# Linear attention and MLP, two layers of each: the denominators' reciprocals of later token chunks spread over the heads by 32-row products

## The chip, the core and the metric

The kernel runs on one core of a Trainium2 chip. The core has five engines with instruction queues of their own: TensorE (PE in the profile; its weight loads are PEld), VectorE (DVE), ScalarE (ACT), GpSimd (POOL) and SyncE (SP, which here issues the transfers). TensorE writes its products into PSUM, in banks of 512 fp32 columns; ScalarE and VectorE take them out to SBUF. The metric is the device time of one execution, in microseconds.

## What is computed

Four layers over x (2048 tokens, 576 features): A, B, A, B, each with a layer norm ahead of it and a residual sum behind it. A is linear attention with 32 heads of 18 features, B is an MLP of width 4608 with a GELU (it normalizes a second time). Cut from the reference:

```python
phi = lambda t: jnp.where(t > 0, t + 1, jnp.exp(t)) + 1e-6
pq, pk = phi(q), phi(k)
kv = jnp.einsum("bhsd,bhse->bhde", pk, v)
z = jnp.einsum("bhsd->bhd", pk)
num = jnp.einsum("bhqd,bhde->bhqe", pq, kv)
den = jnp.einsum("bhqd,bhd->bhq", pq, z)[..., None] + 1e-6
o = num / den                       # then heads side by side, times wo
...
x = x + _A_ref(_layernorm(x, axis=-1), A_wqkv, A_wo)
x = x + _B_ref(_layernorm(x, axis=-1), B_w1, B_b1, B_w2, B_b2)
```

The inputs are bfloat16, and the kernel's products take bfloat16 operands.

## The kernel before, in words

Tokens lie in 16 row tiles of 128, which make four chunks of 512. The 32 heads lie in five groups (`G`): four of 7 heads (126 features) and one of 4 heads (72). The change lies in the last part of layer A (`layer_A`, li = 0 and 2), the output loop at L827 to L846, and in the statistics of the rows that this loop hands to layer B.

*What stands ready ahead of the loop.* `kvwo[g]` holds kv times wo of a group, so that one product per group turns queries into output. The queries are made by `q_proj(g, c)` (L582): five products of 512 columns into one bank, an Exp and an Identity pass of ScalarE, then two VectorE instructions write phi(q) transposed, features by tokens, into `pq[(g, c)]`.

*Denominators.* `den_stage(c)` (L746) makes the denominators of a chunk with 20 products of 32 columns of weights: row tile j of the chunk goes to partitions 32j to 32j+31 (one row a head), 128 tokens along the columns. ScalarE takes Ln and then Exp with a scale of -1, which leaves the reciprocals in `rden` (128x128, one buffer).

*Spread over the heads' features.* `quad_stage(c)` (L765) copies `rden` four times beside each other through a mask, so that row tile j's heads are the only nonzero rows in the j-th 128 columns. `scale_stage(g, c)` (L775) multiplies by the 0/1 matrix `head_bc[:, g, :]`: one full product of 128 rows and 512 columns into a bank, a ScalarE copy to a tile `rden_bc`, and a VectorE multiply of `pq[(g, c)]` by it. This is done for five groups and four chunks.

*Output.* `wo_stage(t)` (L787) makes a row tile's output: ten products of 288 columns (five groups, two halves) into a pair of banks, `accA` and `accB` in turn. `residual` (L501) adds the old x on VectorE (L515) and issues the store of the row tile. SP issues the store, and the loads of old rows by `prefetch_xo`, in the order in which the planner placed them.

*Statistics for layer B.* The first four row tiles go on to layer B's first chunk by way of `LNPipe` (L301), a pipeline whose items move one stage with each `tick`; `hold` delays an item by so many ticks, and the loop ticks twice per row tile up to t = 9. With `stats="act"` ScalarE makes two passes over the row (L333, L340, the group `ln_dump` in the profile); with the default VectorE makes them (`bn_stats`, L349 and L350, and two small instructions). GpSimd makes the power of -1/2, the bias and the normalized row; TensorE then transposes it (L421), not before the output tile `tp_at`, and ScalarE copies it to `yT` (L428).

*What sets the order.* TensorE's instructions in this part are chained in the order of the program text (`pe`, L138). The other engines' orders come from a planner, bound by data and by the orderings without a wait (`add_manual_dep(..., NOSYNC, ...)`). Four PSUM banks, the ring `ps_h`, serve query groups, denominators, spreads and transposes in turn; a new user waits until the user of four places earlier has been read.

`turned` (L110) is an SBUF buffer of 2304 bfloat16 elements a partition, through which layer B's and the next layer's rows are transposed; it is not used during the output loop.

Of the kernel before, what the change touches and what calls it, by code (L numbers as in the profile page):

```python
# [7 lines left out]
ACT = mybir.ActivationFunctionType  # L8
ALU = mybir.AluOpType
BF16 = mybir.dt.bfloat16  # L10
F32 = mybir.dt.float32
# [3 lines left out]
S, D, F, H, DH = 2048, 576, 4608, 32, 18  # L15
P = 128
# [12 lines left out]
CA = 512  # L29
NCA = S // CA  # L30
# [4 lines left out]
def build(tc, A_x, A_wqkv, A_wo, B_w1, B_b1, B_w2, B_b2, out, dbg=None, n_layers=4):  # L35
    nc = tc.nc
    dbg = dbg or {}
    with ExitStack() as ctx:
        const = ctx.enter_context(tc.tile_pool(name="const", bufs=1))
        ps_h = ctx.enter_context(tc.tile_pool(name="ps_h", bufs=4, space=PSUM))  # L40
# [18 lines left out]
        head_bc = const.tile([P, G, P], BF16, name="head_bc")  # L59
# [50 lines left out]
        turned = const.tile([P, D // 32, TPC, 32], BF16, name="turned")  # L110
# [6 lines left out]
        rows = ctx.enter_context(tc.tile_pool(name="rows", bufs=9))  # L117

        def row_tile(name):
            return rows.tile([P, D], F32, name=name, tag="row")  # L120
# [3 lines left out]
        NOSYNC = mybir.DependencyInfo(mybir.DependencyClass.NoSync, mybir.DependencyReason.SCHED_ONLY)  # L124
# [13 lines left out]
        def pe(inst):  # L138
            if pe_chain["on"]:
                if pe_chain["last"] is not None:  # L140
                    tc.add_manual_dep(inst.ins, pe_chain["last"], NOSYNC, reason="TensorE order in the MLP")
                pe_chain["last"] = inst.ins.name
            return inst
# [76 lines left out]
        dve_last = dict(norm=None, sum=None, phi=None)  # L220
# [80 lines left out]
        class LNPipe:  # L301
# [11 lines left out]
            def tick(self, transposes=1):  # L313
                land()
                for it in list(self.items):
# [8 lines left out]
                    if st == -1:  # L324
                        xn = row_tile("xl")
# [4 lines left out]
                    elif st == 0 and it["stats"] == "act":  # L330
                        mv = it["mv"] = work.tile([P, 2], F32, name="ln_mv", bufs=6)
                        it["dump"] = blk.tile([P, D], BF16, name="ln_dump", tag="blk")
                        nc.scalar.activation(out=it["dump"][:], in_=it["xt"][:, 0:D], func=ACT.Identity,  # L333
                                             scale=-1.0 / D, accum_out=mv[:, 0:1])
                        it["stage"] = 0.5
                        continue
                    elif st == 0.5:
                        u = it["u"] = work.tile([P, 1], F32, name="ln_u", bufs=4)
                        mv = it["mv"]
# [6 lines left out]
                    elif st == 0:  # L346
                        xt = it["xt"]
                        stt = work.tile([P, 2, 6], F32, name="ln_st", bufs=4)
                        first = nc.vector.bn_stats(out=stt[:, 0, :], in_=xt[:, 0:HALF])  # L349
                        second = nc.vector.bn_stats(out=stt[:, 1, :], in_=xt[:, HALF:D])  # L350
                        after = dve_last["sum"] if it["after"] == "sum" else it["after"]
# [3 lines left out]
                        mv = work.tile([P, 2], F32, name="ln_mv", bufs=6)  # L355
# [23 lines left out]
                    elif st in (2, 3):  # L379
# [4 lines left out]
                        xt = it["xt"]  # L384
                        if it["norm"] == "act":
                            nc.scalar.activation(out=y[:, 0:D], in_=xt[:, 0:D], func=ACT.Identity,
                                                 scale=it["rstd"][:, 0:1], bias=it["nmr"][:, 0:1])
# [12 lines left out]
                        if it["kind"] == "A" and it["evac"] == "dma":  # L400
                            c, j = divmod(it["t"], TPC)
# [4 lines left out]
                    elif st == 4:  # L406
                        y = it["y"]
                        t = it["t"]
# [6 lines left out]
                        first = it["kind"] == "A" and t < 2  # L415
# [7 lines left out]
                        if first:  # L423
                            act_last["turned"] = nc.scalar.copy(out=yT[:, 0:3, t * P:(t + 1) * P], in_=tp[:, 0:3, :]).ins.name
                            copy = nc.vector.tensor_copy(out=yT[:, 3:KD, t * P:(t + 1) * P], in_=tp2[:, 3:KD, :])
# [16 lines left out]
        lnp = LNPipe()  # L442
        act_last = dict(exp=None, gelu=None)
# [81 lines left out]
        def layer_A(li, next_kind, pre_a1=None):  # L525
# [3 lines left out]
            pq = {}  # L529
# [67 lines left out]
            q_left = [(g, c) for c in range(NCA) for g in range(G)]  # L597
            pe_chain["on"] = True
            kvwo = {}
            if li > 0:  # L600
# [87 lines left out]
                for g in range(G):  # L688
                    pe(nc.tensor.matmul(zp[0:GR[g], g:g + 1], lhsT=k2[4][:, GO[g]:GO[g] + GR[g]], rhs=ident[:, 64:65],
                                        start=True, stop=True))  # L690
# [30 lines left out]
            if li == 0:  # L721
# [5 lines left out]
                                    in1=zp[0:126, 0:4].unsqueeze(2).to_broadcast([126, 4, H]), op=ALU.mult)  # L727
            nc.vector.tensor_tensor(out=zsel[0:72, 4, :], in0=head_sel[0:72, 4, :],
                                    in1=zp[0:72, 4:5].to_broadcast([72, H]), op=ALU.mult)
# [12 lines left out]

            quad_rden = {}
            rden_of = {}

            def den_stage(c, after=None, pair=None):  # L746
                if pair:
                    dp = ps_acc.tile([P, 2, 512], F32, name="den_pair", tag=pair)[:, 0, :]
                else:
                    dp = ps_h.tile([P, 512], F32, name="den_ps", tag="h")  # L750
                for g in range(G):
                    rows = 127 if g == 0 else GR[g]
                    for j in range(TPC):
                        pe(nc.tensor.matmul(dp[32 * j:32 * (j + 1), 0:P], lhsT=zsel[0:rows, g, :],
                                         rhs=pq[(g, c)][0:rows, j * P:(j + 1) * P],
                                         start=(g == 0), stop=(g == G - 1)))
                rden = work.tile([P, P], BF16, name="rden", bufs=1)
                log = nc.scalar.activation(out=dp[:, P:2 * P], in_=dp[:, 0:P], func=ACT.Ln)
                if after is not None:
                    tc.add_manual_dep(log.ins, after, NOSYNC, reason="copies first")  # L760
                act_last["rden"] = nc.scalar.activation(out=rden[:], in_=dp[:, P:2 * P], func=ACT.Exp,
                                                        scale=-1.0).ins.name
                rden_of[c] = rden

            def quad_stage(c, after=None):  # L765
                quad = blk.tile([P, D], BF16, name="quad_rden", tag="blk")
                spread_out = nc.vector.tensor_tensor(
                    out=quad[:, 0:CA].rearrange("p (j n) -> p j n", j=4), in0=quad_mask[:],
                    in1=rden_of.pop(c)[:].unsqueeze(1).to_broadcast([P, 4, P]), op=ALU.mult)
                if after is not None:  # L770
                    tc.add_manual_dep(spread_out.ins, after, NOSYNC, reason="sums first")
                quad_rden[c] = quad
                dve_last["quad"] = spread_out.ins.name

            def scale_stage(g, c, pair=None):  # L775
                if pair:
                    bp = ps_acc.tile([P, 2, 512], F32, name="rden_pair", tag=pair)[:, 0, :]
                else:
                    bp = ps_h.tile([P, 512], F32, name="rden_ps", tag="h")
                pe(nc.tensor.matmul(bp[:, 0:CA], lhsT=head_bc[:, g, :], rhs=quad_rden[c][:, 0:CA], start=True, stop=True))  # L780
                rb = blk.tile([P, D], BF16, name="rden_bc", tag="blk")
                act_last["copy"] = nc.scalar.copy(out=rb[0:GR[g], 0:CA], in_=bp[0:GR[g], :]).ins.name  # L782
                mult = nc.vector.tensor_tensor(out=pq[(g, c)][0:GR[g], 0:CA], in0=pq[(g, c)][0:GR[g], 0:CA],  # L783
                                               in1=rb[0:GR[g], 0:CA], op=ALU.mult)
                dve_last["mult"] = mult.ins.name

            def wo_stage(t):  # L787
                c, j = divmod(t, TPC)
                wp = ps_acc.tile([P, 2, 512], F32, name="wo_ps", tag=("accA", "accB")[t % 2])
                for half in range(2):  # L790
                    for g in range(G):
                        pe(nc.tensor.matmul(wp[:, half, 0:HALF], lhsT=pq[(g, c)][0:GR[g], j * P:(j + 1) * P],  # L792
                                              rhs=kvwo[g][0:GR[g], half * HALF:(half + 1) * HALF],
                                              start=(g == 0), stop=(g == G - 1)))
                xn = residual(li, t, wp[:, :, 0:HALF])
                if xn is not None and next_kind == "B" and t < TPC:
                    lnp.feed(xn, t, "B", "pool", "act", hold=1, stats="act", tp_at=6 + 2 * t)

            for t in range(AHEAD):
                prefetch_xo(li, t, add_b2=False)  # L800
# [9 lines left out]
            if li > 0:  # L810
                kv_groups((2, 3, 4))
                late = [q_proj(*q_left.pop(0), defer=True)]
            kv_wo(2)
            kv_wo(3)
            if li == 0:
                late = [q_proj(*q_left.pop(0), defer=True)]
# [10 lines left out]
            for t in range(NT):  # L827
                c, j = divmod(t, TPC)
                if t + AHEAD < NT:
                    prefetch_xo(li, t + AHEAD, add_b2=False)  # L830
                wo_stage(t)
                for late in list(rden_of):
                    quad_stage(late, after=dve_last["sum"])
                if q_left:
                    q_proj(*q_left.pop(0))
                if c + 1 < NCA:
                    for g in ((0, 1, 2), (3, 4), (), ())[j]:
                        scale_stage(g, c + 1)
                if j == 1 and c + 2 < NCA:
                    den_stage(c + 2)  # L840
                if t == NT - 3:
                    warm_table(ACT.Gelu_apprx_tanh, act_last["copy"])
                state["wo"] = t
                lnp.tick()
                if t < 10:
                    lnp.tick(transposes=0)  # L846
# [237 lines left out]
```

## Time and profile before

| | us |
|---|---|
| median of 3 runs (lowest to highest) | 768.49 (768.37 to 768.53) |
| the profiled execution | 768.48 |
| its span, first to last instruction | 766.7 |
| output loop of li = 0, from its first output product to the MLP's first | 77.68 to 107.32 |
| output loop of li = 2, likewise | 454.07 to 481.70 |
| in these two stretches together (57.26): TensorE busy | 55.80 |
| ScalarE busy | 45.22 |
| VectorE busy | 43.13 |
| GpSimd busy | 18.46 |

The granted TensorE clock is 1.00 in both stretches. A TensorE product's duration in the profile reaches into the time of the next one (a product of 288 columns lasts 286 ns, while products of this kind start 120 to 125 ns apart), so a stretch is read by the starts of its instructions. A line of a timeline has the start in us, the length of the group, engine, line of the kernel, operation, what it writes and reads, shapes, and how many instructions it groups; in brackets the idle time ahead of it and what ended it.

### The profile page before, as it was taken

To read this page: it belongs to the slowest core of one execution; us is meant where nothing else is said; L and a number is where in the kernel's file an instruction comes from. 1 tells how busy PE (TensorE), PEld (TensorE's weight loads), DVE (VectorE), ACT (ScalarE), POOL (GpSimd) and SP (SyncE) were. 2 spreads that over 40 slices of the span, in tenths; PEclk is the share of its full clock that TensorE was granted. 3 is DMA by queue.
4 is the path that set the end of the run, shared out by engine and by line. 5 is a ranking of instruction groups with operands and counts; after the bars stand their busy time and mean duration, and the time that the engine had idled before them with its cause. 6 is when DMAs were issued, how large, how long until landed. Compare 5 with 4: busy or idle time off the path is not lost.

```text
span 766.7 us, 15671 instructions
## 1 busy us (share of the span) xinstructions
PE 760.5 (99%) x6522; PEld 492.6 (64%) x6522; DVE 269.5 (35%) x669; ACT 341.5 (45%) x768; POOL 123.9 (16%) x202
## 2 busy tenths in 40 slices
PE   9999999999999999999999999999999999999998
PEld 6776664675477457646777767447745764674476
DVE  7786764035113603400455677600140032000000
ACT  5888956304710660164056578560065027205600
POOL 4681412012100301200110004300020011001000
PEclk9999999999999999999999999999999999999999
DMA  9992483016402721330246007530131033011000
GB/s 262 264 302 48 140 276 79 28 57 164 123 24 62 194 70 40 96 87 1 73 122 214 1 16 247 203 81 15 51 107 50 17 124 81 9 32 55 2 9 24
DMA packets 80289, 73.82 MB, mean 96 GB/s; under 512 B 36698, under 2 KB 64858, under 8 KB 80218
## 3 DMA queue, kind: packets, MB, share of 16 engines
q1 hardware_dynamic: 80218, 72.82, 32.3%
q8 instruction: 51, 0.84, 0.5%
q14 instruction: 20, 0.16, 0.1%
HBM read 48.03 MB, written 24.77 MB: 95 GB/s over the span
## 4 chain that ended last, share of the span: by engine, by line
PE 96%; ACT 3%; DVE 1%; issue 0%; DMA 0%; ACTq 0%
PE m_ps L965 36%; PE h_ps L907 20%; PE hp_ps L907 16%; PE q_ps L585 5%; PE wo_ps L792 3%; PE k_ps L537 3%; PE k_ps L608 3%; PE k_ps L625 2%; PE v_ps L558 1%; PE m_half L965 1%; PE v_ps L555 1%; ACT rden_bc L782 1%; PE tp L421 1%; ACT ln_dump L333 1%; PE kvacc L579 1%; PE k_tail L625 1%
## 5 line engine op out<-in xcount | busy, mean ns | idle before, releaser
L965 PE MATMUL m_ps<-w_sb,hT 128*128 128x288 bf16 x2232 | 274.8, 286 | 0.0
L965 PEld LDWEIGHTS <-hT 128*128 128x128 bf16 x2304 | 224.8, 98 | 59.8 <-issue 3.4
L907 PEld LDWEIGHTS <-w_sb 64*128 64x128 bf16 x2304 | 124.5, 94 | 136.4 <-issue 1.9
L907 PE MATMUL hp_ps<-yT,w_sb 64*128 64x512 bf16 x1152 | 178.0, 376 | 0.0
L907 PE MATMUL h_ps<-yT,w_sb 64*128 64x512 bf16 x1152 | 147.9, 376 | 0.0
L912 ACT COPY relay_sb<-relay_sb 128x1 f32<-128x1 f32 x144 | 28.6, 198 | 262.9 <-PE h_ps L907 220.0
L903 ACT ACTIVATE hT<-h_ps,b1T 128x512 bf16<-128x512 f32 x144 | 91.2, 684 | 43.8 <-PE h_ps L907 43.8
L372 POOL TENSOR_TENSOR ln_rstd<-ln_u,neg_half 128x1 f32<-128x1 f32 x64 | 36.2, 567 | 376.8 <-DVE ln_u L363 225.6
L903 ACT ACTIVATE hT<-hp_ps,b1T 128x512 bf16<-128x512 f32 x144 | 91.2, 693 | 0.0
L515 DVE TENSOR_TENSOR xbf<-m_ps,xo 128x576 bf16<-128x576 f32 x15 | 11.4, 758 | 214.5 <-PE m_ps L965 214.5
L515 DVE TENSOR_TENSOR xo<-m_ps,xo 128x576 f32<-128x576 f32 x16 | 12.1, 758 | 174.6 <-PE m_ps L965 174.6
L498 POOL TENSOR_TENSOR xo<-xo,b_bc 128x576 f32<-128x576 f32 x32 | 41.0, 1286 | 100.5 <-DMA xo<-x_d 63.6
L907 PE MATMUL h_ps<-yT,w_tail 64*128 64x512 bf16 x144 | 54.1, 376 | 0.0
L907 PE MATMUL hp_ps<-yT,w_tail 64*128 64x512 bf16 x144 | 54.1, 376 | 0.0
L585 PE MATMUL q_ps<-yT,wqkv_sb 128*126 128x512 bf16 (+1 forms) x200 | 49.8, 380 | 0.0
L792 PE MATMUL wo_ps<-kvwo,pq 126*128 126x288 bf16 (+1 forms) x320 | 43.4, 286 | 0.4
L907 PEld LDWEIGHTS <-w_tail 64*128 64x128 bf16 x288 | 27.1, 94 | 17.1
L792 PEld LDWEIGHTS <-pq 126*128 126x128 bf16 (+1 forms) x320 | 30.1, 97 | 10.7 <-DVE pq L783 0.9
L464 ACT ACTIVATE phi_e<-k_ps 128x288 bf16<-128x288 f32 x46 | 19.3, 419 | 38.7 <-PE k_ps L608 35.8
L585 PEld LDWEIGHTS <-wqkv_sb 128*126 128x126 bf16 (+1 forms) x200 | 24.9, 131 | 11.7 <-issue 0.4
L472 DVE TENSOR_SCALAR phi_e<-phi_e 128x288 bf16<-128x288 bf16 (+2 forms) x86 | 24.8, 288 | 19.9 <-ACT phi_e L464 19.2
L464 ACT ACTIVATE phi_e<-q_ps 126x512 bf16<-126x512 f32 (+1 forms) x40 | 23.9, 598 | 17.1 <-PE q_ps L585 16.8
(133 smaller groups left out, 665.4 us busy)
## 6 DMA issues: line engine op xcount, KB each, us to landing
xo<-x_d SPq DMA_DIRECT2D x48, 288.0 KB
x_d<-xo SPq DMA_DIRECT2D x32, 288.0 KB
xl<-x_d SPq DMA_DIRECT2D x24, 288.0 KB
y_d<-turned SPq DMA_DIRECT2D x40, 144.0 KB
w_sb<-in_B_w_dram SPq DMA_DIRECT2D x6, 864.0 KB
yT<-y_d SPq DMA_DIRECT2D x10, 512.0 KB
w_sb<-in_B_w_dram SPq DMA_DIRECT2D x9, 512.0 KB
x_d<-xn SPq DMA_DIRECT2D x16, 288.0 KB
```

The source lines that it names most:

```text
L372: nc.gpsimd.tensor_tensor(out=rstd[:], in0=it["u"][:], in1=neg_half[:], op=ALU.pow)
L464: exp = nc.scalar.activation(out=e_out, in_=ps_ap, func=ACT.Exp)
L472: low = nc.vector.tensor_scalar(out=e[0:rows, 0:n], in0=e[0:rows, 0:n], scalar1=1.0, scalar2=1e-6, op0=ALU.min, op1=ALU.add)
L498: nc.gpsimd.tensor_tensor(out=xo[:], in0=xo[:], in1=b2_bc[:], op=ALU.add)
L515: total = nc.vector.tensor_tensor(out=xn[:, cols].rearrange("p (h n) -> p h n", h=2), in0=halves, in1=xo[:, cols].rearrange("p (h n) -> p ...
L537: pe(nc.tensor.matmul(kp[:, 0:HALF], lhsT=yT[:, k, tok], rhs=wqkv_sb[:, k, D + half * HALF: D + (half + 1) * HALF], start=(k == 0), stop=( ...
L585: pe(nc.tensor.matmul(qp[0:GR[g], :], lhsT=wqkv_sb[:, k, GO[g]:GO[g] + GR[g]], rhs=yT[:, k, c * CA:(c + 1) * CA], start=(k == 0), stop=(k ...
L792: pe(nc.tensor.matmul(wp[:, half, 0:HALF], lhsT=pq[(g, c)][0:GR[g], j * P:(j + 1) * P], rhs=kvwo[g][0:GR[g], half * HALF:(half + 1) * HALF ...
L903: act_last["gelu"] = nc.scalar.activation(out=to, in_=ps, func=ACT.Gelu_apprx_tanh, bias=b1T[:, f:f + 1], scale=1.0).ins.name
L907: mm = pe(nc.tensor.matmul(dst[n], lhsT=wt, rhs=mv, start=(seen[n] == 0), stop=(seen[n] == 8)))
L912: relay = nc.scalar.copy(out=relay_sb[:, 1:2], in_=relay_sb[:, 0:1])
L965: pe(nc.tensor.matmul(acc[half][:, 0:HALF], lhsT=hT[f][:, j * P:(j + 1) * P], rhs=w2_sb[:, f, half * HALF:(half + 1) * HALF], start=(f == ...
```

## The change

1. *Spread.* For chunks 1 to 3 groups 0 to 3 are no longer spread by `scale_stage`. A new `quarter_stage(c)` multiplies `rden` directly: for each group and each quarter i of the partitions, a product of 32 rows and 128 columns, quarter i into bank i, all four banks of the ring at once. ScalarE then copies each bank into a part of `turned`. `quarter_scale` multiplies `pq` of a group by four runs of 128 columns from the four parts. Group 4 and all of chunk 0 keep `scale_stage`, and so `quad_stage` stays.
2. *Order.* The spread of chunk 1 stands after output tile 1, those of chunks 2 and 3 after tiles 3 and 7; the denominators of chunk 2 move from tile 1 to tile 2, those of chunk 3 stay at tile 5. Multiplies of `pq` and masked spreads are placed behind a row tile's residual sum.
3. *Statistics.* The first four row tiles' statistics start later (`hold` 4, 4, 6, 8 in place of 1). Those of tiles 1 and 3 go to VectorE behind the latest sum, those of tiles 0 and 2 stay on ScalarE behind the latest Exp of the denominators.
4. *Queries.* Query groups left for the loop (three in li = 0, one in li = 2) are not issued at tiles 1 and 3, where spreads stand.

```diff
@@ LNPipe.tick, statistics on ScalarE
-                        nc.scalar.activation(out=it["dump"][:], in_=it["xt"][:, 0:D], func=ACT.Identity,
-                                             scale=-1.0 / D, accum_out=mv[:, 0:1])
+                        one = nc.scalar.activation(out=it["dump"][:], in_=it["xt"][:, 0:D], func=ACT.Identity,
+                                                   scale=-1.0 / D, accum_out=mv[:, 0:1])
+                        if it["after"] == "rden":
+                            tc.add_manual_dep(one.ins, act_last["rden"], NOSYNC, reason="denominators first")
@@ den_stage
                 rden_of[c] = rden
+                rden_now["tile"] = rden
@@ new
+            def quarter_stage(c):
+
+                rden = rden_now["tile"]
+                banks = [ps_h.tile([P, 512], F32, name="rden_ps", tag="h") for _ in range(4)]
+                for g in range(4):
+                    for i in range(4):
+                        rows = slice(32 * i, 32 * (i + 1))
+                        pe(nc.tensor.matmul(banks[i][0:126, g * P:(g + 1) * P], lhsT=head_bc[rows, g, 0:126],
+                                            rhs=rden[rows, :], start=True, stop=True))
+                spread_rows = turned[:].rearrange("p a t c -> p (a t c)").rearrange("p (i w) -> p i w", i=4)
+                for i in range(4):
+                    act_last["copy"] = nc.scalar.copy(out=spread_rows[0:126, i, 0:4 * P], in_=banks[i][0:126, :]).ins.name
+
+            def quarter_scale(c, groups, after):
+                spread_rows = turned[:].rearrange("p a t c -> p (a t c)").rearrange("p (i w) -> p i w", i=4)
+                for g in groups:
+                    scaled = pq[(g, c)][0:126, 0:CA].rearrange("p (i n) -> p i n", i=4)
+                    mult = nc.vector.tensor_tensor(out=scaled, in0=scaled,
+                                                   in1=spread_rows[0:126, :, g * P:(g + 1) * P], op=ALU.mult)
+                    tc.add_manual_dep(mult.ins, after, NOSYNC, reason="sums first")
+                    dve_last["mult"] = mult.ins.name
@@ wo_stage
-                    lnp.feed(xn, t, "B", "pool", "act", hold=1, stats="act", tp_at=6 + 2 * t)
+                    lnp.feed(xn, t, "B", "pool", "act", hold=(4, 4, 6, 8)[t], tp_at=6 + 2 * t,
+                             **(dict(after="sum") if t % 2 else dict(stats="act", after="rden")))
@@ the output loop, behind wo_stage(t)
-                for late in list(rden_of):
-                    quad_stage(late, after=dve_last["sum"])
-                if q_left:
+                total = dve_last["sum"]
+                if c + 1 < NCA:
+                    for g in ((), (), (0, 1, 2, 3), ())[j] if c == 0 else ((0, 1), (2, 3), (), ())[j]:
+                        quarter_scale(c + 1, (g,), after=total)
+                    if t == 1:
+                        quarter_stage(1)
+                    if j == 3 and c + 2 < NCA:
+                        quarter_stage(c + 2)
+                    if j == (2 if c == 0 else 0):
+                        scale_stage(4, c + 1)
+                if j == (2 if c == 0 else 1) and c + 2 < NCA:
+                    den_stage(c + 2)
+                    if c > 0:
+                        quad_stage(c + 2, after=total)
+                if t == 3:
+                    quad_stage(2, after=total)
+                if q_left and t not in (1, 3):
                     q_proj(*q_left.pop(0))
-                if c + 1 < NCA:
-                    for g in ((0, 1, 2), (3, 4), (), ())[j]:
-                        scale_stage(g, c + 1)
-                if j == 1 and c + 2 < NCA:
-                    den_stage(c + 2)
```

More of the change, by code (lines that the diff above doesn't have):

```diff
@@ L744, in layer_A @@
             rden_of = {}
+            rden_now = {}
             def den_stage(c, after=None, pair=None):
```

## The prediction, made before the changed kernel ran

> **What bounds the kernel.** I read the page first: which engine is full, and what its chain of waits holds.
>
> ```profile
> PE 760.5 (99%) x6522; PEld 492.6 (64%) x6522; DVE 269.5 (35%) x669; ACT 341.5 (45%) x768; POOL 123.9 (16%) x202
> ...
> PE 96%; ACT 3%; DVE 1%; issue 0%; DMA 0%; ACTq 0%
> ```
>
> TensorE is the bound, but 3% of the chain stands on ScalarE. Comparing the two programs' instruction orders shows that the change touches only the output loops of the two attention layers (li=0: 77.68 to 107.32; li=2: 454.07 to 481.70), so I read TensorE's timeline there, li=2 first:
>
> ```profile
> 454.07 1.71 PE L792 MATMUL wo_ps<-kvwo,pq 126*128 126x288 bf16 x10
> 455.62 1.24 PE L585 MATMUL q_ps<-yT,wqkv_sb 128*72 128x512 bf16 x5
> ...
> 458.58 0.60 PE L780 MATMUL rden_ps<-quad_rden,head_bc 128*128 128x512 bf16 x2
> 459.11 0.47 PE L754 MATMUL den_ps<-pq,zsel 127*32 127x128 bf16 x20
> 459.50 4.11 PE L792 MATMUL wo_ps<-kvwo,pq 126*128 126x288 bf16 x30
> 463.45 0.81 PE L780 MATMUL rden_ps<-quad_rden,head_bc 128*128 128x512 bf16 x3
> ...
> 465.34 0.38 PE L780 MATMUL rden_ps<-quad_rden,head_bc 128*128 128x512 bf16 x1
> 466.17 0.38 PE L780 MATMUL rden_ps<-quad_rden,head_bc 128*128 128x512 bf16 x1 [0.46 <-ACT rden_bc L782]
> 466.66 0.47 PE L754 MATMUL den_ps<-pq,zsel 127*32 127x128 bf16 x20
> ```
>
> The starts matter, since each duration holds a tail that overlaps the next product. The paces: a broadcast (0.81−0.38)/2 = 0.216 us; a query group of five 1.08; a row tile's ten output products 1.235 (ten rows start that far apart elsewhere in the loop); five transposes 0.28. Against them the starts lose 0.32 before the first query group, 0.10 at 459.11, 0.25 within the 30 products, 0.61 between 465.34 and 466.17, 0.27 before 466.66: 1.55. In li=0 the same sum gives 1.5, of which again 0.32 stands before the loop's first steps and is not touched. ScalarE's timeline tells why:
>
> ```profile
> 464.11 0.79 ACT L340 ACTIVATE ln_dump<-xo,ln_mv 128x576 bf16<-128x576 f32 x1
> ...
> 464.87 0.69 ACT L333 ACTIVATE ln_dump<-xo 128x576 bf16<-128x576 f32 x1
> ...
> 465.53 1.56 ACT L782 CAST rden_bc<-rden_ps 126x512 bf16<-126x512 f32 x3
> ```
>
> Broadcasts issued from 463.45 on are evicted only from 465.53, behind passes over statistics. So about 1.2 us a layer is ScalarE's, and the rest of the loop is TensorE's own work.
>
> **Part by part.** *The spread.* Per later chunk (three a layer) four full 128-row products of 512 columns go: 4×0.216 = 0.86 us. In come 16 products of 32 rows and 128 columns, four row quarters into four banks. No 32-row product is in this trace. The nearest row is the denominators' 20, four column quarters wide and also 128 columns long:
>
> ```profile
> 76.97 0.38 PE L780 MATMUL rden_ps<-quad_rden,head_bc 128*128 128x512 bf16 x1
> 77.28 0.47 PE L754 MATMUL den_pair<-pq,zsel 127*32 127x128 bf16 x20
> 77.68 1.71 PE L792 MATMUL wo_ps<-kvwo,pq 126*128 126x288 bf16 x10
> ```
>
> Their starts spread over 0.47−0.22 = 0.25 us: five waves of four, 0.06 apart, so four run at once. From 76.97+0.216 to 77.68 the whole step takes 0.49, so about 0.20 goes at entering and leaving the quarter shape. Four waves then cost 0.24+0.20 = 0.44. That row quarters run at once too is carried by the MLP's 64-row halves (L907 in the page: 2,592 products of 512 columns, 560 us in a row at 0.216; the chain of waits gives them 20% and 16%, 276 us). Lower end 0.37, were the change of shape a third cheaper; upper ends in the rivals. I take 0.44: a saving of 0.42 a chunk, 6×0.42 = 2.5 us, all on the path.
>
> The Trainium skill, TensorE: Matmul & The Clock Gate, section "Wait — 56ns, not 53.3ns?", says that starts never come closer than about 25 ns; 16 starts would then take 0.40 and the step 0.60. The 13 ns above disagrees, and the measurement decides.
>
> *Evictions and multiplies.* ScalarE still makes four 126x512 copies a chunk (0.48 apart: (1.56−0.60)/2), into `turned` in place of four tiles; VectorE still makes five multiplies and one masked spread. I cost the multiplies alike at 0.34 apart (83.12 0.75 x2). Their new operand comes in four runs of 128; the masked spread, whose operand is also read in four runs, takes 0.43 like them. Not one multiply can start before all four copies are done, a new wait: that is in the walk below. Reuse of `turned` makes a chunk's copies wait for the last chunk's multiplies.
>
> *Statistics.* Of eight ScalarE passes a layer four go: 2×(0.67+0.76) = 2.9 us of ScalarE. VectorE gets two rows' statistics of about 1.2 us (two halves of 0.44, 0.21, 0.14). The remaining passes are held behind a denominators' Exp. *Queries* are not issued beside a spread; the group of five is moved, not changed. *SP* issues the same 308 transfers; in li=2 stores and loads change places and the load of row 10 waits for row 1's normalization; I place that near 467 with row 10 added near 473, so it has 4 us where its issue takes 0.32. GpSimd has no new work.
>
> *The walk.* All four PSUM banks of one ring go to a spread, and the next broadcast, denominators or query group must take them back in order, one copy at a time. I laid the new order out with these paces.
>
> li=2: first spread 457.93 (after two output tiles), copies 458.45 to 460.48, multiplies of chunk 1 to 461.95. Denominators 459.82, their Exp done 461.43; second spread enters 461.55; output tile 4 at 461.99, its operands ready. ScalarE makes the two passes first, copies of chunk 2 from 462.77: the single broadcast waits for a bank and the masked spread, 463.22 to 463.45, 0.23 lost. Third spread 468.15 (about 0.1 more lost on a sum), its copies 468.67 to 470.7, well ahead of tile 12 at 474.3. MLP at 479.6 in place of 481.70: 2.1 us less.
>
> li=0 has two more query groups in the loop. First spread 81.54, no wait; second 86.23, 0.1 for the last query bank. Chunk 2's copies start at 87.59 behind two query passes and two statistics passes; the broadcast loses 0.34, the query group 0.26, and the third denominators 0.18 for that query. MLP at 105.9 in place of 107.32: 1.4 us less.
>
> So the saving of 2.5 is joined by 2.3 us of old waits that end and eaten by 1.3 us of new ones (0.9 in li=0, 0.4 in li=2, rounded up): 2.5+2.3−1.3 = 3.5. The profiled execution took 768.48 (span 766.7 and 1.8 around it; the median shown is 768.49), so **765.0**. What comes late next is the bank ring, by ScalarE's four copies in a row. The MLP's input cannot be late: its last transposes stand three output tiles (3.7 us) ahead of it, as before. Own range of this case: 763.8 to 766.6, for 0.3 us a layer either way in bank waits and a spread of 0.37 to 0.60.
>
> **Rivals.**
> *All new waits vanish*: the gain is 2.5+2.3, 763.7, and with a spread of 0.37 763.3. For it, chunks 1 and 3 find their banks free in the walk; against it, chunk 2's copies stand behind 1.4 us of statistics. 0.10.
>
> *Loads do not hide within a row quarter*: each wave pays a load and then a product. A load of 126 columns is bounded by z_ps (L689, five one-column products in 0.47−0.20, 0.07 each), so a wave is 0.13, the spread 4×0.13+0.20 = 0.72, 6×0.28 = 1.7 us less gain: 766.7. Against it, the denominators' second wave of loads starts while the first wave's products run (20 loads busy 0.29 us in all). The Trainium skill's same page, section "The mechanism", has this rule: a load overlaps products in flight only in another row group. The trace's denominators, which use all rows, disagree. 0.12.
>
> *VectorE becomes the bound*: at the sums' rate (0.76 for 576 fp32) a strided multiply takes 0.60 apart. Twelve of them a layer push everything behind them back. In li=2 chunk 1's are done at 462.9 in place of 461.95 (tile 4 waits 0.55, the masked spread brings that to 0.85), and then the sums of tiles 5 and 6 hold tiles 7 and 8 up to 2.1 in all; in li=0 the third denominators wait 1.3 for a query. Together 3.4: 768.4, no change. The masked spread's 0.43 speaks against it. 0.10.
>
> *Slower: products in series.* If the four quarters do not overlap, 16 products go singly. At the pace of kv_ps (L645, 126 by 126, 0.0575) a spread is 1.12; 6×(1.12−0.86)−1.0 = +0.6: 769.1, 0.05. If load and product also follow each other, 0.13 each, the spread is 16×0.13+0.20 = 2.28: 6×1.42−1.0 = +7.5: 776.0, 0.10. It decides from a spread of about 1.03 us on, where 6×0.17 eats the 1.0 net of waits. For it: no row shows four row quarters at once. Against: the halves do overlap.
>
> **How the numbers follow.** Forecast 0.53, the rivals 0.10, 0.12, 0.10, 0.05, 0.10. The range 763.2 to 768.4 takes in all but the series (0.05+0.10). A measurement of this kernel tells about 0.2%, 1.5 us, from no change. Faster (below 767.0): 0.53+0.10 and most of 0.12, 0.74; same 0.16; slower 0.10.
>
> **What would show it.** The spread's 16 products start over some 0.2 us, and the next output product starts 0.44 after the last one's end; over 0.9 there means series. The MLP starts near 105.9 and some 25.6 us after 454.07. No broadcast waits behind `ln_dump`; waits in front of single broadcasts are for `turned` copies, 0.2 to 0.4 each. VectorE's multiplies from `turned` last 0.43; at 0.6 or more VectorE is the bound. If the spread shows 0.44 and the loops end no earlier, the bank ring has taken the gain.

## The result, and the profile after

| | before | after |
|---|---|---|
| median (lowest to highest, 6 runs each), us | 768.51 (768.33 to 768.66) | 771.94 (769.55 to 772.55) |
| the profiled execution, its span, us | 768.48, 766.72 | 769.55, 767.84 |
| loop of li = 0, first output product to the MLP, us | 29.64 | 28.78 |
| loop of li = 2, likewise, us | 27.64 | 29.59 |

The ratio is 1.0042, 95% interval 1.0032 to 1.0052. The change makes the kernel **slower by 0.4%**; the prediction was 765.0, faster, with a range up to 768.4. The loops account for the profiled execution: −0.86 and +1.95 make +1.09, and the span grew by 1.12. The other five executions of the changed kernel took 2.2 to 3.0 us more than the profiled one. All five had a mean granted clock of 0.996 to 0.998, the profiled one 1.000; that part is taken up below.

In the changed kernel the line numbers are other ones: output products are L818, the spread by quarters L798, broadcasts L784, the row sums L517; of the transfers, L524 is the store of a row tile and L495 the load of an old one. The first two fences are the busy times and the chain of waits of the page after:

```profile
PE 758.3 (99%) x6594; PEld 491.6 (64%) x6594; DVE 270.0 (35%) x685; ACT 336.9 (44%) x752; POOL 124.0 (16%) x198
```

```profile
PE 95%; DMA 2%; DVE 2%; ACT 1%; issue 0%; SPq 0%; DVEq 0%
```

ScalarE's share of the chain fell from 3% to 1%, which is what the change was forecast to do. In its place stand transfers (2%), which were at 0%. TensorE's timeline of li = 2 after the change shows where:

```profile
453.24 1.71 PE L818 MATMUL wo_ps<-kvwo,pq 126*128 126x288 bf16 x10
...
455.87 1.40 PE L818 MATMUL wo_ps<-kvwo,pq 126*128 126x288 bf16 x10
457.19 0.45 PE L798 MATMUL rden_ps<-rden,head_bc 32*126 32x128 bf16 x16
457.57 1.41 PE L818 MATMUL wo_ps<-kvwo,pq 126*128 126x288 bf16 x10
...
461.24 1.41 PE L818 MATMUL wo_ps<-kvwo,pq 126*128 126x288 bf16 x10
462.74 0.38 PE L784 MATMUL rden_ps<-quad_rden,head_bc 128*128 128x512 bf16 x1
...
474.86 0.44 PE L423 MATMUL tp<-ident,y_ring 128*128 128x128 bf16 x5
476.51 1.39 PE L818 MATMUL wo_ps<-kvwo,pq 126*128 126x288 bf16 x10 [1.20 <-DVE xo L517]
480.21 2.68 PE L818 MATMUL wo_ps<-kvwo,pq 126*128 126x288 bf16 x20 [2.31 <-DVE xo L517]
482.82 1.04 PE L943 MATMUL h_ps<-yT,w_sb 64*128 64x512 bf16 x8
```

Up to 474.86 the stretch runs as the walk had it. The spread takes 0.38 from its first start to the next output product, and some 0.09 at entry (455.87 to 457.19 is 1.32, where ten output products pace 1.235). Then TensorE stands still twice ahead of the last three output tiles (13, and 14 with 15), behind row sums on VectorE. No such wait was in the profile before. Starts show what each stop costs: the ten products at 476.51 could have begun 0.28 after the transposes at 474.86, so 1.37 is lost; those at 480.21 could have begun 1.235 after 476.51, so 2.47 is lost. Without these 3.84 the MLP would have begun at 478.98, 25.74 us after the loop's first product; the prediction said 25.6.

Why were the sums late? They add the *old* row, which has to be loaded first. SP's timeline of the changed kernel (stores L524 and loads L495, in SP's order; a time here is how long SP was held at the instruction):

```profile
459.80 2.73 SPq L524 DMA_DIRECT2D x_d<-xo  x2
464.53 3.67 SPq L495 DMA_DIRECT2D xo<-x_d  x2
468.29 0.85 SPq L524 DMA_DIRECT2D x_d<-xo  x2
472.51 0.32 SPq L495 DMA_DIRECT2D xo<-x_d  x1
472.88 0.90 SPq L524 DMA_DIRECT2D x_d<-xo  x2
473.88 1.26 SPq L495 DMA_DIRECT2D xo<-x_d  x2
```

The second line holds the loads of rows 9 and 10. Row 10's takes the buffer of row 1, which is free only when GpSimd has normalized row 1, at 467.8. SP works in order, so the stores of row tiles 4 and 5, whose sums end at 464.4 and 466.1, go out only at 468.29. Store 4 lands at 472.49; the load of row 11 takes that store's buffer and cannot go earlier than 472.51. Row 12's load takes the buffer of store 5, and stores 6 and 7 and the load of row 13 stand in the queue behind row 11's. From there the loads come close behind each other, as the chain of waits in order of time shows (excerpt):

```profile
468.29 4.20 DMA x_d<-xo
...
473.88 5.40 DMA xo<-x_d
...
480.21 2.68 PE wo_ps L818 x20
```

The load at 473.88 is row 12's; it lands 5.40 us after its issue. VectorE's timeline has the sums of rows 10, 11 and 12:

```profile
472.62 0.74 DVE L517 TENSOR_TENSOR xo<-wo_ps,xo 128x576 f32<-128x576 f32 x1
475.70 0.76 DVE L517 TENSOR_TENSOR xo<-wo_ps,xo 128x576 f32<-128x576 f32 x1 [2.33 <-PE tp L423]
479.39 0.76 DVE L517 TENSOR_TENSOR xo<-wo_ps,xo 128x576 f32<-128x576 f32 x1 [2.94 <-DMA xo<-x_d]
```

Row 10 itself is not late: its load goes out at 467.87, lands at 471.77, and its sum starts at 472.62 without a wait. Row 11's sum waits for its load, which lands at 475.62 (the bracket names the transposes, which had ended by 475.3), and row 12's for the load of 473.88.

The same seen from the transfers, in two stretches of li = 2 (columns: stretch and length, busy time and instructions of PE, PEld, DVE, ACT and POOL, granted clock, DMA share, GB/s). Before the change:

```profile
464.00:472.00 8.00, 7.43 (x78) 5.17 (x76) 6.11 (x11) 6.37 (x18) 6.77 (x16) 1.00 0.63 178
472.00:480.00 8.00, 8.00 (x72) 6.27 (x70) 5.88 (x11) 5.45 (x10) 0.97 (x2) 1.00 1.04 382
```

and after it:

```profile
464.00:472.00 8.00, 8.00 (x100) 6.00 (x99) 7.93 (x20) 7.28 (x16) 7.02 (x14) 1.00 0.48 147
472.00:480.00 8.00, 4.70 (x43) 3.60 (x41) 2.73 (x6) 1.97 (x4) 1.63 (x2) 1.00 0.80 233
```

Before, the transfers ran at a full share (1.04) in the last 8 us of the loop. After, they moved less in both stretches, and not for want of room. In slices of 0.4 us from 464.00 to 480.00 their busy share is, in tenths:

```profile
DMA  0003794000009269999400049489999965898999
```

They stand idle from 466.8 to 468.8, when SP waits for row 1, and from 472.0 to 473.2, when it waits for store 4. What is then released comes close together, and each load lands later than the one ahead of it: 3.1 us after its issue for row 11, 5.4 for row 12, 6.2 for row 13.

### The profile page after: what moved, and what is told of

Read it like the earlier page. It is cut to its first block, busy times and chain, and to the rows that moved or that the text cites. A ratio compares the mean times of both kernels' runs of the same rounds, so it can differ in the third digit from the quotient of the medians.

```text
span 767.8 us, 15791 instructions
## 1 busy us (share of the span) xinstructions
PE 758.3 (99%) x6594; PEld 491.6 (64%) x6594; DVE 270.0 (35%) x685; ACT 336.9 (44%) x752; POOL 124.0 (16%) x198
## 4 chain that ended last, share of the span: by engine, by line
PE 95%; DMA 2%; DVE 2%; ACT 1%; issue 0%; SPq 0%; DVEq 0%
PE m_ps L1001 36%; PE h_ps L943 20%; PE hp_ps L943 16%; PE q_ps L587 5%; PE wo_ps L818 3%; PE k_ps L539 3%; PE k_ps L610 3%; PE k_ps L627 2%; PE v_ps L560 1%; PE m_half L1001 1%; PE v_ps L557 1%; DMA xo<-x_d 1%; DMA wqkv_sb<-in_A_wqkv_dram 1%; PE tp L423 1%; DMA x_d<-xo 1%; PE kvacc L581 1%
## 5 line engine op out<-in xcount | busy, mean ns | idle before, releaser
L517 DVE TENSOR_TENSOR xbf<-m_ps,xo 128x576 bf16<-128x576 f32 x15 | 11.4, 758 | 212.7 <-PE m_ps L1001 212.7
L517 DVE TENSOR_TENSOR xo<-m_ps,xo 128x576 f32<-128x576 f32 x16 | 12.1, 758 | 173.7 <-PE m_ps L1001 173.7
L818 PE MATMUL wo_ps<-kvwo,pq 126*128 126x288 bf16 (+1 forms) x320 | 44.0, 286 | 3.8 <-DVE xo L517 3.5
L818 PEld LDWEIGHTS <-pq 126*128 126x128 bf16 (+1 forms) x320 | 29.8, 97 | 13.6 <-issue 3.8
```

Source lines behind the costliest of these rows:

```text
L517: total = nc.vector.tensor_tensor(out=xn[:, cols].rearrange("p (h n) -> p h n", h=2), in0=halves, in1=xo[:, cols].rearrange("p (h n) -> p ...
```

## Experiments

Two theories stood against each other. **A**: the loss is the place of stores 4 and 5 in SP's queue, behind the load that waits for row 1; the spread and the statistics do what the walk said. **B**: the spread, the multiplies or the statistics cost more than priced, and the row waits are only where it shows. A second question was why most executions lose another 2.2 to 3.0 us.

**The changed kernel once more, one execution.**

> The changed kernel as it is, for a trace of an execution whose granted clock falls. Theory A: the clock falls to a lower value within a few us of the row waits near 480, and the products after it run slower for some us; 771.5 to 772.5. If the clock stays at 1.000: 769.5 and nothing new. Rival C: the fall lies elsewhere, in the first attention layer's loop or without idle time ahead of it.

It took 773.46 (span 771.75), above the 771.5 to 772.5 expected; the clock falls where theory A put it. TensorE's timeline and the clock by stretches:

```profile
477.84 1.39 PE L818 MATMUL wo_ps<-kvwo,pq 126*128 126x288 bf16 x10 [2.21 <-DVE xo L517]
481.63 4.96 PE L818 MATMUL wo_ps<-kvwo,pq 126*128 126x288 bf16 x20 [2.40 <-DVE xo L517]
```

```profile
480.00:485.00 5.00, 3.37 (x15) 2.07 (x15) 2.23 (x3) 0.00 (x0) 0.00 (x0) 0.52 1.04 398
485.00:490.00 5.00, 5.00 (x39) 2.22 (x39) 1.98 (x6) 0.63 (x3) 0.01 (x1) 0.80 0.90 304
```

The granted clock is at half from 480.16 for 6.83 us, and the same 20 output products take 4.96 in place of 2.68. Half speed for 6.83 us of 772 is a mean clock of 0.996, the value of four of the five longer executions; 0.998 is half of that stretch. So the waits are paid twice: once as idle time, and again by a slower array behind it.

**All stores ahead of the loads that follow them.** Only SP's order differs; the instruction orders of the other four engines are those of the changed kernel.

```diff
-        sp_last = dict(turned=None, landed=None)
+        sp_last = dict(turned=None, landed=None, stored=None)
-                behind(load, "landed")
+                behind(load, "stored" if t > AHEAD else "landed")
-            nc.sync.dma_start(out=x_d[t], in_=xn)
+            sp_last["stored"] = nc.sync.dma_start(out=x_d[t], in_=xn).ins.name
```

> The changed kernel, but in the second attention layer's output loop SP issues the load of an old row t behind the store of row t-5; TensorE, VectorE, ScalarE and GpSimd keep their instruction orders. Theory A (late rows): stores 4 and 5 no longer stand behind row 10's load, rows 11 to 13 land in time, the loop takes 25.7 us from its first output product to the MLP's first in place of 29.6, the span is 764.0 and the time 765.7 to 766.2, at a granted clock of 1.000 in every run. Rival B (the transfers have no room in a loop that is 2 us shorter, whatever their order): 2 us or more of waits for rows stay, 767.5 to 769.6. Rival C (the clock falls because of the 32-row products, not of idle time): the clock stays near 0.996 in most runs and the time is some 2.4 us above what the profile's waits explain.

Measured: 766.14 (765.42 to 766.86), ratio to before 0.9973 [0.9963, 0.9983], and 765.70 when it was run again (below). All its runs had a granted clock of 1.000. SP now sends store 5 ahead of row 10's load (466.01 and 467.71), and the loads stay spread out:

```profile
464.23 0.32 SPq L524 DMA_DIRECT2D x_d<-xo  x1
464.66 0.38 SPq L495 DMA_DIRECT2D xo<-x_d  x1
466.01 0.32 SPq L524 DMA_DIRECT2D x_d<-xo  x1
467.71 0.32 SPq L495 DMA_DIRECT2D xo<-x_d  x1
```

li = 2 takes 26.45 (25.7 was expected), with 0.75 of row waits left; li = 0 is unchanged at 28.78. A holds: 5.8 us between the two medians with no work added or removed.

**Stores 4 and 5 alone ahead of row 10's load** (`"stored" if t == 10 else "landed"`), every other transfer as in the changed kernel.

> The changed kernel with the stores of row tiles 4 and 5 issued ahead of row 10's load; nothing else in SP's order, and no other engine's order, is different. Theory A (the whole loss is that queue place): store 4 goes out near 464.5 instead of 468.29, its ring buffer is free near 468, the loads of rows 11 to 13 no longer bunch, and the two waits of the output products for row sums in li=2 (1.20 and 2.31) fall under 0.5 each; the loop of li=2 takes 26 to 26.7 us, no stretch at half clock, and the time is 765.3 to 766.6, like the run with all stores first (766.14). Rival (the loads are late for another reason, such as the number of transfers in the loop or the late normalization of row 1 alone): at least 2 us of row waits remain, 768 or more.

Measured: 765.65 (764.80 to 767.10), ratio 0.9963 [0.9949, 0.9977]; li = 2 in 26.69. Both waits were expected to fall under 0.5; one of 0.57 is left (0.74 by the starts), and 0.26 within the products ahead of it. Still, these two stores alone bring back all that moving every store did. No run moved only one of them.

**A control: the kernel before with stores first.**

> A control: the kernel before with the same rule for SP (each store ahead of the load issued after it), all else as before; no other engine's order is different. The kernel before has no output product that waits for a row sum in li=2, so by theory A there is nothing to gain: 768.0 to 768.8, ratio 0.999 to 1.001. Rival: the 2.1 us by which the changed kernel with stores first beats the kernel before come partly from the order of the transfers by itself: 767.5 or less here.

Measured: 768.35 beside 768.20 of before, ratio 1.0002 [0.9993, 1.0011]. The order of the stores is worth nothing where no row is late. What the two kernels above gain over before is the change's own gain, with the two stores out of the way.

**Statistics alone** (part 3 put into the kernel before; spreads, order and queries as before).

> The kernel before with part 3 alone: later statistics, two of the four rows' on VectorE; spreads by full products, order and queries as before. My walk: the waits behind statistics passes end, 1.2 us a layer, or up to 2.3 us in all, 766.0 to 767. The loop of li=2 near 26.5 us, that of li=0 near 28.6, if the rows stay in time: SP's order here has the store of row 4 ahead of row 10's load. Rival: the late normalization of row 1 is enough by itself to make old rows late: row waits of 2 us or more in li=2, 768.5 or more.

Measured: 767.33, ratio 0.9990 [0.9981, 1.0000], just above the 766.0 to 767 expected. li = 2 takes 26.60, that is 1.04 less, with no wait on ScalarE and no row wait: in this kernel's order store 4 stands ahead of row 10's load, which fits theory A. li = 0 takes 29.80, 0.16 more: a new wait of 0.89 on a row sum, whose output buffer GpSimd's normalization held, eats the 1.0 there.

**The spread without the statistics** (`feed(..., hold=1, stats="act")` as before, all else as changed).

> The changed kernel with the statistics of before (all four rows on ScalarE, hold 1). Theory A: rows 0 to 3 are normalized sooner and SP's loads spread out again, so row waits fall under 1 us, while ScalarE's 2.9 us a layer come back in front of the copies and cost bank waits; 766 to 768, clock 1.000. Rival B (the shorter loop itself makes rows late): row waits of 3 us and more stay, 769 to 772. Rival D (the later statistics brought no gain at all): 765.5 or less.

Measured: 772.19, ratio 1.0043 [1.0027, 1.0060]. I missed by 4 us and more. The rows are in time, as A says (li = 2 takes 27.69 without a row wait), but ScalarE's passes stand ahead of queries and spread copies again, and now there are four copies in one piece behind them. TensorE's timeline in li = 0:

```profile
95.04 0.24 PE L757 MATMUL den_ps<-pq,zsel 72*32 72x128 bf16 x4 [2.31 <-DVE pq L478]
95.21 1.40 PE L818 MATMUL wo_ps<-kvwo,pq 126*128 126x288 bf16 x10
96.46 0.65 PE L423 MATMUL tp<-ident,y_ring 128*128 128x128 bf16 x5
96.90 2.60 PE L818 MATMUL wo_ps<-kvwo,pq 126*128 126x288 bf16 x10
```

li = 0 takes 33.43. Ten output products take 2.60 at 96.90 because the clock is at half for 3.41 us from 96.54, after one idle time of 2.5; the one execution at a clock of 1.000 took 770.08, still more than before. So part 3 is not an addition to part 1; the spread needs it.

**The idle time filled.** The changed kernel with 6 and 12 products that nobody reads, ahead of output tiles 13 and 14 of li = 2: more work for TensorE, and the same wait for rows.

```diff
+                if li > 0 and t in (13, 14):
+                    fill = ps_h.tile([P, 512], F32, name="fill_ps", tag="h")
+                    for _ in range(6 if t == 13 else 12):
+                        pe(nc.tensor.matmul(fill[:], lhsT=w1_sb[:, 0, 0:P], rhs=w1_sb[:, 0, 0:512],
+                                            start=True, stop=True))
```

> The changed kernel with 6 and 12 products of 512 columns that nobody reads, put on TensorE ahead of output tiles 13 and 14 of the second attention layer, where it waits 1.4 and 2.5 us for rows; 1.3 and 2.6 us of work. Theory A (the clock falls because TensorE stands idle there): clock 1.000 in every run and 769.4 to 770.0, like the one run of the changed kernel at clock 1.000. Rival C (the fall has another cause): 771.5 to 772.5 at clock 0.996 in most runs.

Measured: 770.18 (769.47 to 770.82), just above the 769.4 to 770.0 expected and 1.8 us *less* than the changed kernel, with a clock of 0.999 or 1.000 in all ten runs, though its loop of li = 2 is longer (30.84 against 29.59). That separates the two costs: about 1 us of lost time in the loops, as in the profiled execution, and some 2.5 us of lost clock in the executions where it falls.

**Products of a spread quarter by quarter**, four of one row quarter in a row in place of four quarters in turn, on the kernel with stores first.

```diff
-                for g in range(4):
-                    for i in range(4):
+                for i in range(4):
+                    for g in range(4):
```

> The kernel with the stores first (766.14), but the 16 products of a spread go quarter by quarter: four products of one row quarter (and one bank) in a row, then the next quarter's. Same products, same operands. Theory (four row quarters run at once only when they are issued in turn): the 16 products go nearly singly, at 0.0575 each, a spread takes about 1.1 us in place of 0.475, six of them cost 2.5 to 3.8 us, less what waits for banks take in: 768 to 770. Rival (the order within a spread does not matter, the array starts each product as soon as its own quarter is free and the queue looks ahead): 766.1, the spread 0.48.

Measured: 765.91, ratio 0.9975 [0.9964, 0.9985]: no difference. One of its eight executions took 768.63, at a clock of 0.998, and left no trace. My theory that quarters overlap only when issued in turn falls. TensorE's timeline of this kernel:

```profile
460.63 0.48 PE L798 MATMUL rden_ps<-rden,head_bc 32*126 32x128 bf16 x16
461.04 1.41 PE L818 MATMUL wo_ps<-kvwo,pq 126*128 126x288 bf16 x10
```

From the spread's first start to the next output product it is 0.41 here and 0.38 with the quarters in turn. In series at the 0.0575 of `kv_ps` it would be 0.92 for the sixteen.

**Queries beside the spreads** (part 4 undone: `if q_left:`), on the kernel with stores first.

> The kernel with the stores first (766.14), with part 4 of the change undone: in li=0 the three query groups left for the loop are issued at the first three opportunities, tiles 1 and 3 (spreads) among them. li=2 hardly differs. By my walk the spread and the query group then compete for the four banks of the ring: 0.3 to 1 us more in li=0's loop (28.78 us with the queries apart), 766.4 to 767.2. Rival: bank waits only move, li=0's loop stays within 0.2 us of 28.78, 766.1.

Measured: 766.90, ratio 0.9983 [0.9973, 0.9992]; li = 0 in 29.52, 0.74 more than 28.78; li = 2 as it was (26.46). The wait is where the walk put it, a query group behind the spread's copies, and a row sum's wait comes to it:

```profile
83.19 1.24 PE L587 MATMUL q_ps<-yT,wqkv_sb 128*126 128x512 bf16 x5 [0.66 <-ACT turned L802]
...
96.62 1.39 PE L818 MATMUL wo_ps<-kvwo,pq 126*128 126x288 bf16 x10 [0.71 <-DVE xn L517]
```

**Two tries at the waits that remain**, by the holds of the first rows' statistics, and the kernel with stores first again beside them: row 1 earlier (4, 2, 6, 8), and with it row 0 later (6, 2, 6, 8).

> The kernel with the stores first (766.14), and the statistics of row 1 held 2 ticks in place of 4, those of row 2 and 3 as they were (holds 4, 2, 6, 8): row 1's normalization frees its buffer earlier, so that the load of row 10 can be issued near 465.5 in place of 467.71. The 0.75 us of row waits that are left in li=2 should go, 765.5, if VectorE has room for 1.2 us of statistics ahead of the masked spread; if not, the masked spread is late by about 1 us, and the broadcast behind it gives back 0.3 to 0.6 us in each layer: 766 to 767.

> As the kernel with row 1 earlier, and row 0's passes on ScalarE held 6 ticks in place of 4, so that they no longer stand ahead of chunk 2's four copies (holds 6, 2, 6, 8). Theory: the waits for these copies (0.42 and 0.27 us in li=0, 0.26 in li=2) shrink by about half, 0.3 to 0.5 us less, 765 to 765.5. Rival: row 0's buffer is free later, row 9's load is late in place of row 10's, and the row waits of li=2 come back with 0.5 us or more: 766 or over.

> The kernel with the stores first once more, beside the two with other holds on the same chip: 765.4 to 766.9 as before, ratio 0.997 to before.

Measured: 768.54, ratio 1.0000 [0.9991, 1.0009]; 771.68, ratio 1.0045 [1.0032, 1.0058]; and 765.70, ratio 0.9967 [0.9954, 0.9979]. Both tries lose: at most 767 was expected of the first and 765 to 765.5 of the second, 766 or over by its rival. In the first the row waits of li = 2 are gone, as expected, but the statistics stand ahead of the masked spread, and GpSimd, serving row 1 too, is late with row 0:

```profile
464.40 0.39 PE L784 MATMUL rden_ps<-quad_rden,head_bc 128*128 128x512 bf16 x1 [0.71 <-DVE ln_u L368]
...
468.94 0.58 PE L423 MATMUL tp<-ident,y_ring 128*128 128x128 bf16 x5 [1.18 <-POOL y_ring L391]
```

In the second the transposes of row 0 wait 2.75 for GpSimd, which neither the theory nor its rival had, and the clock falls for 3.41 us at 471.3. Of all kernels tried, those with stores sent first and the holds of the change are the best, 765.65 to 766.14, and the measurements do not tell them apart.

## Why the prediction was wrong

**The step that failed** is the sentence on SP: "I place that near 467 with row 10 added near 473, so it has 4 us where its issue takes 0.32." It put the change of places between stores and loads at nothing. For row 10 that came out: its load was issued at 467.87 and added at 472.62 without a wait. That the room sufficed was luck, since a load needs the time to its landing, 3.90 here, and not the 0.32 of its issue; in the kernel with all stores first it took 5.31, and the sum of row 10 waited 0.68. What failed is that I looked only at the load that waits, not at what stands behind it on an engine that works in order: stores 4 and 5, which went out 3.9 and 2.6 us after their sums, through their buffers the loads of rows 11 and 12, and behind those row 13's. The price is 3.84 us of idle time in li = 2, plus what the clock then takes. In the list of what would show the steps I had no sign for a row sum.

**The slower rival** had the sign and not the mechanism. It had the quarters in series; they overlap, and sixteen starts lie within 0.23 us. That its 769.1 lies near the profiled 769.55 is chance.

**The other steps, by their own terms:**
- *The spread*, 0.44 forecast: 0.47 with its entry, 0.50 once. Right, and in its parts: 0.23 of starts and some 0.24 for entering and leaving.
- *Multiplies from four runs*, 0.43 alone: two in 0.74 and four in 1.43 by VectorE's timeline, as before. VectorE did not become the bound.
- *ScalarE's waits go*: yes, but they were put a little high. In li = 2 the statistics alone were worth 1.04, where some 1.2 was read: the 0.09 ahead of each denominators' step is still there in that run. In the changed kernel no product of TensorE's waits for VectorE's statistics. The spread needs the later statistics, as the run without them shows.
- *li = 2*, 2.1 less forecast: 1.9 less without the row waits.
- *li = 0*, 1.4 less forecast: 0.86. Waits for banks and for the query were put at 0.88 (0.1, 0.34, 0.26, 0.18); they measure 0.05, 0.42, 0.27 and 0.41, 0.27 more in all. The three spreads add 0.1. The last thirty output products take 3.80 up to the MLP, before as after, where the walk's pace makes 3.71: 0.09 more. Under 0.1 stays open.

With the two stores out of the way the sum comes out near the forecast: 765.65 to 766.14 against 765.0. The 0.6 to 1.1 that is missing lies in the 0.5 of li = 0 and the row waits of 0.75 to 1.0 that remain in li = 2.

**The clock** was not in the prediction at all. The profile before had it at 1.00 throughout, and no step of mine made an idle time as long as these. A forecast that adds idle time to a busy TensorE should ask for this second cost.

## What to carry to other kernels

When a change makes one instruction wait on an engine that works in order, list everything that its queue holds behind it, and follow each buffer that these free; count transfers to their landing, not to their issue. And an idle time of some 2.5 us on TensorE can cost another 1.7 us in clock, half of 3.41: before judging a new order by one profile, look at the granted clock of every run.

## What the runs showed of the hardware

- *The clock falls after idle times shorter than I would have thought, and by windows.* One stop of 2.5 us (start to start) and one of 3.0 were each followed, about 1.5 and 1 us after they ended, by 3.41 us at half clock. Stops of 2.43 and 2.68 with ten products between them brought 6.83 us; in the profiled execution of the same program, stops of 1.42 and 2.60 brought none. The Trainium skill, TensorE: Matmul & The Clock Gate, section "What's actually happening", gives half clock after an idle window of about 3.4 us, in windows that run freely. The windows agree: counted from the clock's first rise in a trace, the three falls lie at 27, 139 and 136 times 3.413 us (4.38 to 96.54, 5.71 to 480.16, 7.09 to 471.30). That a window needs to be wholly idle does not: no stop here was 3.4 us long. With the traces cut into these windows, TensorE's busy time in a window tells what follows:

| trace | window, us | TensorE busy in it, us | clock behind it |
|---|---|---|---|
| row 0 later | 467.89 to 471.30 | 1.01 | half |
| changed kernel once more | 476.75 to 480.16 | 1.39 | half |
| spread without the statistics | 93.13 to 96.54 | 1.50 | half |
| changed kernel, profiled | 478.37 to 481.78 | 1.57 | full |
| changed kernel, profiled | 474.96 to 478.37 | 1.74 | full |

In every trace kept, the clock fell behind each window at full clock with 1.50 us or less and behind none with 1.57 or more. So whether a stop costs clock depends also on where the windows lie over it. No run was made to test this border. Two executions at a clock of 0.998 left no trace to look at, 768.63 of the spread quarter by quarter and one of the kernel before, 770.22; the traces kept of these two kernels have no stop of this size, so these falls stay unexplained.
- *Row quarters seem to have queues of their own.* With quarters in turn, the four products of a wave start 3 ns apart, the second wave 0.106 us after the first, and the next two 0.057 after the one ahead. Issued quarter by quarter, the sixteen start in four groups at the same distances, at steps of 13 ns within a group, 0.26 us in all. The trace doesn't name a product's quarter, so this is argued: the first product of each quarter is then the 1st, 5th, 9th and 13th to be issued, and four issues at 3.3 ns make 13 ns, as if each quarter's four went into a queue of their own and ran beside the others. The Trainium skill's same page, section "The mechanism", agrees on starts some 4 ns apart across row groups; it also has products start strictly in program order, which sixteen starts in 0.26 us with four 128-column products per quarter in a row would hardly allow.
